# Attention with a GELU layer on one core: exponentials of later sets laid out by key block, value tiles cut at 224 queries, and a plan with new lengths

## The chip, the cores and the metric

The kernel runs on one core of a Trainium2 chip. The metric is the device time of one execution in microseconds (us); the median of nine runs before the change is 333.05 us (332.61 to 334.46). The core's engines work side by side, each with its own queue of instructions in order: TensorE (PE) multiplies matrices, VectorE (DVE) and ScalarE (ACT) work elementwise, GpSimd (POOL) applies masks and issues most loads, SyncE (SP) issues stores. An engine waits for another by a semaphore. Results of TensorE land in PSUM, which has eight banks of 512 four-byte columns on each of 128 partitions; this kernel gives four to scores and four to a ring that all other products share.

## The reference

`q`, `k`, `v` have 8 batches, 8 heads, 576 queries and 64 features; 16 "beacon" keys and values stand ahead of the 576 keys.

```python
k_all = np.concatenate([beacon_k, k], axis=2)          # 592 keys
v_all = np.concatenate([beacon_v, v], axis=2)
scores = np.matmul(q, k_all.transpose(0, 1, 3, 2)) / sqrt(64)
causal[:, 16:] = np.triu(np.ones((576, 576), dtype=bool), k=1)
scores = np.where(causal, -1000000000.0, scores)
a = np.exp(scores - scores.max(-1, keepdims=True))
a /= a.sum(-1, keepdims=True) + 1e-09
attn = np.matmul(a, v_all)                              # joined to (4608, 512)
h = x @ w_in                                            # (512, 2048)
g = h * (1.0 / (1.0 + np.exp(-1.702 * h)))
out = g @ w_out                                         # (2048, 512)
```

## The kernel before

**Sets.** Four heads of one batch make a *set*; there are 16 (`NSET`), two to a batch. Set s uses four 32-row or 32-column parts of TensorE at once, one for each head. The 592 keys are cut in five *blocks* of 128 (the last has 80). By causality block j concerns queries from `s0s[j]` = 0, 112, 240, 368, 496 on, so a head has 576 + 464 + 336 + 208 + 80 = 1664 columns of exponentials.

**Exponentials.** They lie in `E` (4 heads x 1664 columns) in the order of `PIECES`: first all blocks for queries 0 to 287, then all blocks for queries 288 to 575. The columns are computed in *chunks* of up to 512 (`CHUNKS`): scores (`e_qk`, L429, op `qk`), one ScalarE exponential for each set in it (`e_exp`, L447). There is a single score buffer, so chunk i+1 is computed once chunk i has been read. The triangles on the diagonal are masked in place (`e_mask`, L457; mostly on GpSimd). Sets 0 to 3 (`s < EARLY`) take their chunks by halves of queries; later sets run through the 1664 columns 512 at a time, a chunk often holding the end of one set and the start of the next.

**Sums and values.** For a later set VectorE adds the blocks' exponentials up (`e_zadd`, L484: six adds into `zs`), and a matmul with ones makes row sums (tile x = 2 of `e_av`, L504). Their reciprocal is made by transpose, reciprocal, transpose (`e_z1`, `e_z2`, L532 and L537). Values are matmuls of `E` with every second feature of `v` (x = 0 and 1), one tile for each x and half of the queries, and `e_norm` (L550) multiplies a tile with the reciprocals into `xT`. A set so opens six ring banks: two of sums and four of values. `avS.x.half` names these tiles.

**The GELU layer.** Groups of 256 (groups 0 and 1) and 512 tokens (groups 2 to 9) are multiplied with `w_in` (`e_m1`, L566, op `m1`), one ring bank for each tile. Groups 0 and 1 use a tanh on ScalarE and a gate on VectorE (L607); from group 2 on a GELU table is loaded on ScalarE (L598), and back for the next exponential. Groups 2 to 9 multiply with `w_out` by seven products of quarters (`e_prod`, L677, op `m2`), with sums of quarters on VectorE (`e_s`; `e_t` for the weights, op `t`) and joins (`e_join`, L704); groups 0 and 1 directly (`e_m2`, L619).

**The order.** `Plan` (L28) is a list scheduler that runs while the kernel is built: each operation has an engine, a length written in the kernel, a priority, and for some a due time; `LAT` is the time from an engine's end to another's start. It takes operations in order of the simulated time, and `choose` (L191) selects among TensorE's. `QUOTAS` says how many chunks must have been planned before the first products of a group may begin; `NEAR` lets VectorE wait for an urgent operation. Only the resulting order is in the program: on the chip each engine runs its list as soon as its semaphores allow. Loads of `q`, `k` and `v` are issued from GpSimd's queue, between the masks (`pool_load`, L730); `turns` (L777) transposes a set's queries and keys on VectorE; `values` (L832) and `mlp` (L1000) record the rest.

Of the kernel before, what the change touches and what calls it, by code (L numbers as in the profile page):

```python
# [13 lines left out]
NEAR = 260  # L14
# [9 lines left out]
class Plan:  # L24
# [3 lines left out]
    LAT = {"PE": 230, "ACT": 100, "DVE": 135, "POOL": 60, "Q": 1400, "SP": 0}  # L28
# [35 lines left out]
    def run(self):  # L64
# [33 lines left out]
        while todo:  # L98
# [23 lines left out]
            t, e = best  # L122
            ok = []
# [48 lines left out]
            for u in o.users:  # L172
                u.left -= 1
                lat = self.LAT[o.eng] if u.eng != o.eng or o.eng in ("Q", "DVE", "POOL", "ACT") else 0
                if u.eng == "Q":
                    lat = 300 if o.eng == "SP" else 1200
                elif o.name == "bk" and o.eng != "DVE":
                    lat = 2500
                u.ready = max(u.ready, o.end + lat)
                if u.left == 0:  # L180
                    avail[u.eng].append(u)
# [3 lines left out]
    def choose(self, ok, t, mode, last, free, inside):  # L185
# [15 lines left out]
        late = first(("av",), lambda o: o.ready + 6000 <= t)  # L201
# [11 lines left out]
def kernel(  # L213
# [51 lines left out]
    QUOTAS = (20, 26, 32, 41, 48, 55, 55, 55)  # L265
# [45 lines left out]
    def where(j, a):  # L311
        for (jj, qa, qe), col in zip(PIECES, ecol):
            if jj == j and qa <= a < qe:
                return col + a - qa

    DVM = (0, 1, 2)
    EARLY, ZSUM = 2 * HS, 2 * HS
# [97 lines left out]
    def qk_pieces(i):  # L415
        got, o = [], 0
        for (s, c0, c1) in CHUNKS[i]:
            for (j, a, e), col in zip(PIECES, ecol):
                u, v = max(c0, col), min(c1, col + e - a)
                if u < v:  # L420
                    got.append((v - u, s, j, a + u - col, o))
                    o += v - u
# [34 lines left out]
    def e_mask(s, j, a, e, eng):  # L457
        w = e - a
        col = where(j, a)
# [22 lines left out]
    ZW = HF - Z0  # L482

    def e_zadd(s, i):  # L484
        E = Es[s]
        if s not in zsum:
            zsum[s] = zp.tile([P, Q, ZW + HF], F16, tag="zs", name="zs")
        t = zsum[s]
        if i == 0:
            o, w, x, y = 0, ZW, E[:, :, Z0:HF], E[:, :, ecol[1] : ecol[1] + ZW]  # L490
        elif i == 1:
            w = HF - s0s[2]
            o = ZW - w
            x, y = t[:, :, o : o + w], E[:, :, ecol[2] : ecol[2] + w]
        elif i == 2:
            o, w, x, y = ZW, HF, E[:, :, ecol[3] : ecol[3] + HF], E[:, :, ecol[4] : ecol[4] + HF]
        else:
            j, a, e = PIECES[i + 2]
            w = e - a
            o = ZW + HF - w  # L500
            x, y = t[:, :, o : o + w], E[:, :, ecol[i + 2] : ecol[i + 2] + w]
        nc.vector.tensor_tensor(out=t[:, :, o : o + w], in0=x, in1=y, op=ALU.add)  # L502

    def e_av(s, x, half):  # L504
        b, hs = divmod(s, HS)
        u = ring_tile(("av", s, x, half))
        E = Es[s]
        q0 = half * HF
        terms = []
        if x == 2 and s >= ZSUM:  # L510
            if half == 0:
                terms.append((P, Z0, HF, zsum[s], 0, True, True))
                terms.append((P, 32, Z0, E, 32, True, True))
                terms.append((P, 0, 32, E, 0, True, True))
            else:
                terms.append((P, 0, HF, zsum[s], ZW, True, True))
        else:
            n = len(AVP[half])
            for i, (j, a, e) in enumerate(AVP[half]):
                terms.append((min(P, NK - j * P), a - q0, e - q0, E, where(j, a), i == 0, i == n - 1, j))  # L520
        for kw, a, e, src, col, first, last, *j in terms:
            for h in range(Q):
                lhs = ones[0:kw, :] if x == 2 else vb[b % NB2][0:kw, j[0], Q * hs + h, x::2]
# [8 lines left out]
    def e_z1(s, half):  # L532
        zt = zp.tile([P, HF], F32, tag="zt", name="zt")
        zs[(s, half)] = [zt]
        nc.vector.transpose(out=zt[:, :], in_=rings[("av", s, 2, half)][:, 0:HF])  # L535

    def e_z2(s, half):  # L537
        zt = zs[(s, half)][0]
        rc = zp.tile([P, HF // 32], F32, tag="rc", name="rc")
        nc.vector.reciprocal(  # L540
            out=rc[:, :], in_=zt[:, :].rearrange("p (b k) -> p b k", k=32)[:, :, 0]
        )
        rz = zp.tile([P, HF], F32, tag="rz", name="rz")
        nc.vector.transpose(
            out=rz[:, :].rearrange("p (b k) -> p b k", k=32),
            in_=rc[:, :].rearrange("p (b o) -> p b o", o=1).to_broadcast([P, HF // 32, 32]),
# [3 lines left out]
    def e_norm(s, x, half):  # L550
        b, hs = divmod(s, HS)
        t0 = (b * S + half * HF) % XR
        nc.vector.tensor_tensor(  # L553
            out=xT[:, 2 * hs + x, t0 : t0 + HF],
            in0=rings[("av", s, x, half)][:, 0:HF],
            in1=zs[(s, half)][1][:, :],
# [162 lines left out]
    T_ATT0, T_ATT1 = 13000, 245000  # L719
# [57 lines left out]
    def turns(s):  # L777
        urgent = s < HS
        cast = op(
            "DVE", 80, ld_bk[s] + [turn.get((s - 2, 1))], lambda: e_bk(s),  # L780
# [3 lines left out]
        for which in (1, 0):  # L784
            deps = [ld_qk[(s, which)], cast if which else None]
            turn[(s, which)] = op(
                "DVE", 1095 + 140 * which, deps + [qks[i] for i in CH_OF.get(s - NB2, [])],
                lambda which=which: e_turn(s, which),
                pr=0 if urgent else 4, due=max(0, due_of(s) - 9000), name=f"turn{s}",
            )  # L790

    def chunk(i):
# [14 lines left out]
        for n, (s, c0, c1) in enumerate(CHUNKS[i]):  # L807
            x = exps[(i, n)] = op(
                "ACT", 140 + 0.833 * 4 * (c1 - c0), [qks[i]], lambda n=n: e_exp(i, n), pr=0, name=f"exp{s}.{i}",
# [3 lines left out]
            for m, (j, a, e) in enumerate(MASKS):  # L813
                col = where(j, a)
                if c0 < col + e - a <= c1:
                    eng = "DVE" if s < HS and m in DVM else "POOL"
                    d = 130 + 4 * (e - a) / 1.92 if eng == "DVE" else 270 + 0.71 * 4 * (e - a)
# [10 lines left out]
    zseq += [(s, h ^ (s >= ZSUM)) for s in range(HS, NSET) for h in range(2)]  # L828
# [5 lines left out]
    def values(s):  # L834
        b, hs = divmod(s, HS)
        whole = s >= ZSUM
        order = [(2, 1), (2, 0), (0, 0), (1, 0), (0, 1), (1, 1)] if whole else [
# [4 lines left out]
        if whole:  # L842
            for i, w in enumerate((ZW, HF - s0s[2], HF, HF, S - s0s[3], S - s0s[4])):
                if i in (0, 2):
                    cols = [(ecol[i], ecol[i] + HF), (ecol[i + 1], ecol[i + 1] + HF)]
                    if i == 0:
                        cols = [(Z0, HF), (ecol[1], ecol[2])]
                    else:
                        cols = [(ecol[3], ecol[4]), (ecol[4], ecol[5])]
                else:  # L850
                    k = 2 if i == 1 else i + 2
                    cols = [(ecol[k], ecol[k] + w)]
                sums.append(
                    op(
                        "DVE", 80 + 0.55 * 4 * w, [x for u, v in cols for x in after(s, u, v)] + sums[-1:],
                        lambda i=i: e_zadd(s, i), pr=3, name="zadd",
                    )
                )
        for n, (x, half) in enumerate(order):
            deps = after(s, 0, ETOT) if whole else after(s, half * EHALF, ETOT if half else EHALF)  # L860
            if x < 2:
                deps += [vload[(b, j)] for (j, _, _) in AVP[half]] + [vload[(b, -1)]] + old
                deps += [z2[h] for h in range(2) if whole]
                deps += [avs[(s, 2, half)]]
            w = [e - a for (_, a, e) in AVP[half]]
            if x == 2 and whole:
                deps += sums
                w = [HF] if half else [ZW, Z0 - 32, 32]
# [6 lines left out]
            )  # L875
            if x == 2:
                z1 = op("DVE", 410, [avs[(s, x, half)]], lambda h=half: e_z1(s, h), pr=0, closes=key, name="z1")
                z2[half] = op("DVE", 600, [z1] + [norms.get((*two_back(s, half), y)) for y in range(2)], lambda h=half: e_z2(s, h), pr=0, name="z2")
            else:
                norms[(s, half, x)] = op(  # L880
                    "DVE", 380, [avs[(s, x, half)], z2[half]], lambda x=x, half=half: e_norm(s, x, half),
# [40 lines left out]
    SQ, SDVE, TDUE = 2, 0, 65000  # L922

    def weights():
        prev = []
        for i in range(4):
            prev = [op("DVE", 1450, w2_ld + (prev if i < 3 else [tds[0]]), lambda i=i: e_t(i, "DVE"), pr=3, due=TDUE, name="t")]
# [4 lines left out]
    def products(g):  # L932
        eng = "POOL" if g < SDVE else "DVE"
        sd = {}
        for n0 in range(0, HN, SQ):
            n1 = n0 + SQ
            prev = []
            for i in range(4):
# [3 lines left out]
                d = 150 + 1.0 * 256 * SQ if eng == "POOL" else 70 + 0.675 * 256 * SQ  # L942
# [25 lines left out]
        def join(p, src, dst, deps=(), closes=True):  # L968
            return op(
                "DVE", 620, [last[p]] + list(deps), lambda: e_join(g, p, src, dst), pr=2,  # L970
# [7 lines left out]
        half = op("ACT", 560, [last[1], ends.get(g - 1)], lambda: e_half(g, 1, "m"), pr=1, closes=("p", g, 1), name="half")  # L978
# [19 lines left out]
    def mlp(g):  # L998
# [5 lines left out]
        for hb in range(t0 // HF, (t1 - 1) // HF + 1):  # L1004
            b, half = divmod(hb, 2)
            for hs in range(HS):
                for x in range(2):
                    xs.append(norms[(HS * b + hs, half, x)])
# [5 lines left out]
        for n0 in firsts:  # L1014
# [7 lines left out]
            if g >= GEL:  # L1022
                gates[(g, n0)] = op(
                    "ACT", 555, [pe], lambda n0=n0, n1=n1: e_gelu(g, n0, n1),
# [3 lines left out]
            a = op("ACT", 555, [pe], lambda n0=n0, n1=n1: e_tanh(g, n0, n1), pr=1, name="tanh", table="e")  # L1028
            gates[(g, n0)] = op(
                "DVE", 610, [a], lambda n0=n0, n1=n1: e_gate(g, n0, n1), pr=2, closes=key, name="gate"  # L1030
# [4 lines left out]
        for mt in range(w // P):  # L1035
# [10 lines left out]
            ev = op("ACT", 560, [prev], lambda g=g, mt=mt: e_evac(g, mt), pr=1, closes=key, name="evac")  # L1046
# [61 lines left out]
```

## Time and profile before

| | us |
|---|---|
| median of nine runs | 333.05 |
| the profiled execution: its own time | 333.51 |
| its span in the profile | 331.8 |
| PE busy, of the span | 311.7 (94%) |
| DVE, ACT, POOL busy | 239.9, 202.9, 117.2 |
| 0 to 20 us: PE, DVE busy | 8.2, 11.7 |
| 20 to 68 us: PE, DVE busy | 45.3, 35.7 |
| 68 to 110 us | 41.2, 37.1 |
| 110 to 160 us | 49.7, 41.7 |
| 160 to 215 us | 55.0, 47.9 |
| 215 to 265 us | 49.4, 40.2 |
| 265 to 331.8 us | 62.9, 25.5 |

The profile shows one execution. A group is all instructions of one line and shape, with busy time, mean length of one in ns, and the idle time ahead of them with the engine that ended it. "L439" is a line of the kernel. A timeline row gives start, length, engine, line, operation, tile and count; matmuls overlap, so from row to row the starts say more than the lengths. The granted clock of TensorE is full in the whole span (0.998). The attention ends at 265 us; the rest is the last groups' products.

### The profile page before, as it was taken

The page shows a single profiled execution, that of the slowest core. Times are in us where ns is not written, and L with a number is a line of the kernel's source. Part 1 is how long each engine was busy: PE and PEld are TensorE (multiplying, and loading weights), DVE is VectorE, ACT ScalarE, POOL GpSimd, SP SyncE. Part 2 cuts the span into 40 slices and gives each one's busy share as a digit, 9 for nine tenths or more (in the row PEclk, how much of TensorE's full clock was granted, in tenths as well). Part 3 has the DMA queues.
Part 4 walks back from the last instruction along what each step waited for, and adds up shares of the span by engine and source line. Part 5 has one row for each costly group of instructions (what it writes and reads, how often), then busy time and mean ns, then how long its engine had stood idle before and what let it go on. Part 6 is the DMA issues. An engine that isn't in the chain of part 4 may idle for free.

```text
span 331.8 us, 10414 instructions
## 1 busy us (share of the span) xinstructions
PE 311.7 (94%) x4552; PEld 215.2 (65%) x4552; DVE 239.9 (72%) x514; ACT 202.9 (61%) x234; POOL 117.2 (35%) x190
## 2 busy tenths in 40 slices
PE   0599898999999999999999999999999999999995
PEld 0476566544786468645888888557865546846884
DVE  3846957898799779977899688977988600460483
ACT  1585586776866776778668576957676465065000
POOL 8765675382154606640556044702430000000000
PEclk9999999999999999999999999999999999999999
DMA  7999999449052915390449501920020000210122
GB/s 123 161 205 208 201 177 188 67 61 155 2 114 91 113 33 105 77 166 3 60 95 156 112 34 45 186 16 2 34 97 2 2 0 2 71 60 0 64 96 95
DMA packets 58221, 28.85 MB, mean 87 GB/s; under 512 B 41280, under 2 KB 53568, under 8 KB 58176
## 3 DMA queue, kind: packets, MB, share of 16 engines
q0 software_dynamic: 47552, 18.49, 47.4%
q1 hardware_dynamic: 10560, 9.69, 9.0%
q8 instruction: 35, 0.57, 0.7%
q14 instruction: 10, 0.08, 0.1%
q10 hardware_dynamic: 64, 0.01, 0.0%
HBM read 37.22 MB, written 9.44 MB: 141 GB/s over the span
## 4 chain that ended last, share of the span: by engine, by line
PE 70%; DMA 10%; issue 7%; POOL 5%; ACT 4%; DVE 3%; POOLq 0%; DVEq 0%
PE u L577 29%; PE u L691 25%; PE u L524 7%; PE s L439 6%; DMA w<-in_moe_w_in_dram 5%; DMA w<-in_moe_w_out_dram 5%; ACT E L450 3%; PE u L622 3%; POOL E L471 1%; DVE osb L707 1%; DVE zs L502 1%; POOL vb L370 1%; ACT L598 1%; POOL kn L354 1%; POOL qn L354 1%
## 5 line engine op out<-in xcount | busy, mean ns | idle before, releaser
L577 PE MATMUL u<-xT,w 128*128 128x512 f16 (+1 forms) x704 | 130.7, 342 | 1.5 <-ACT g L598 1.1
L450 ACT ACTIVATE E<-s 128x2048 f16<-128x2048 f32 (+4 forms) x66 | 98.8, 1514 | 51.1 <-PE s L439 50.4
L577 PEld LDWEIGHTS <-w 128*128 128x128 f16 x704 | 67.4, 98 | 57.0 <-issue 2.6
L598 ACT ACTIVATE g<-u 128x512 f16<-128x512 f32 x128 | 74.4, 599 | 46.0 <-PE u L577 31.7
L471 POOL TENSOR_SCALAR_AFFINE_SELECT E<-E 128x512 f16<-128x512 f16 (+3 forms) x90 | 52.6, 611 | 120.2 <-ACT E L450 118.2
L707 DVE SCALAR_TENSOR_TENSOR osb<-u,osb 128x512 f32<-128x512 f32 x56 | 37.7, 681 | 39.7 <-issue 26.5
L691 PEld LDWEIGHTS <-g 128*128 128x128 f16 x512 | 48.8, 98 | 7.0
L439 PE MATMUL s<-qT,kT 32*128 32x32 f16 (+9 forms) x1544 | 35.7, 226 | 13.2 <-DVE qT L410 11.8
L439 PEld LDWEIGHTS <-kT 32*128 32x128 f16 x1544 | 28.7, 95 | 27.7 <-issue 15.2
L691 PE MATMUL u<-w,g 128*128 128x256 f16 x384 | 46.0, 273 | 0.0
L691 PEld LDWEIGHTS <-sA 128*128 128x128 f16 x384 | 36.1, 98 | 5.3
L691 PE MATMUL u<-tB,sA 128*128 128x256 f16 x256 | 32.2, 273 | 0.0
L502 DVE TENSOR_TENSOR zs<-zs,E 128x192 f16<-128x192 f16 (+3 forms) x48 | 27.6, 574 | 3.1 <-POOL E L471 1.5
L524 PE MATMUL u<-E,vb 128*32 128x288 f16 (+4 forms) x1024 | 28.5, 257 | 0.3 <-DVE xT L553 0.3
L370 POOL DMA_DIRECT2D vb<-in_v_dram x32 | 27.3, 867 | 3.6 <-DMA kn<-in_k_dram 1.8
L553 DVE TENSOR_TENSOR xT<-u,rz 128x288 f16<-128x288 f32 x64 | 26.0, 449 | 1.7 <-PE u L524 1.2
L410 DVE STREAM_TRANSPOSE kT<-kn 128x576 f32<-128x576 f32 x16 | 20.1, 1257 | 6.8 <-DMA kn<-in_k_dram 3.2
L524 PEld LDWEIGHTS <-vb 128*32 128x32 f16 (+1 forms) x1024 | 21.9, 98 | 4.6 <-issue 1.7
L642 DVE TENSOR_TENSOR sA<-g 128x512 f16<-128x512 f16 x32 | 13.1, 427 | 14.5 <-ACT g L598 14.5
L410 DVE STREAM_TRANSPOSE qT<-qn 128x576 f32<-128x576 f32 x16 | 19.9, 1244 | 0.9 <-PE s L439 0.5
L535 DVE STREAM_TRANSPOSE zt<-u 128x288 f32<-128x288 f32 x32 | 13.9, 463 | 7.0 <-PE u L524 6.7
L502 DVE TENSOR_TENSOR zs<-E 128x704 f16<-128x704 f16 (+1 forms) x24 | 16.4, 682 | 1.3 <-POOL E L471 1.1
(44 smaller groups left out, 230.7 us busy)
## 6 DMA issues: line engine op xcount, KB each, us to landing
out_dram<-osb SPq DMA_DIRECT2D x36, 256.0 KB, 2.5
kn<-in_k_dram POOLq DMA_DIRECT2D x16, 288.0 KB, 6.5
qn<-in_q_dram POOLq DMA_DIRECT2D x16, 288.0 KB, 6.1
vb<-in_v_dram POOLq DMA_DIRECT2D x24, 128.0 KB, 5.6
w<-in_moe_w_in_dram POOLq DMA_DIRECT2D x8, 256.0 KB, 8.7
w<-in_moe_w_out_dram POOLq DMA_DIRECT2D x4, 512.0 KB, 14.0
vb<-in_v_dram POOLq DMA_DIRECT2D x8, 112.0 KB, 4.7
vb<-in_v_dram POOLq DMA_DIRECT2D x8, 80.0 KB, 5.7
```

What stands on the lines that cost most here:

```text
L370: nc.gpsimd.dma_start(out=t[0 : hi - lo, j, h0:h1, :], in_=v[b, h0:h1, lo:hi, :].rearrange("h n d -> n h d"),)
L410: nc.vector.transpose(out=f32(dst.rearrange("p n e -> p (n e)")).rearrange("p (r t) -> p t r", t=TR), in_=f32(src[:, :]).rearrange("p (t c ...
L439: nc.tensor.matmul(sc[:, h, o : o + w], kT[s % NB2][r : r + 32, j * P : (j + 1) * P, d], qT[s % NB2][r : r + 32, a : a + w, d], start=(d = ...
L450: nc.scalar.activation(out=Es[s][:, :, c0:c1], in_=ss[i][:, :, o : o + c1 - c0], func=AFT.Exp, scale=0.125,)
L471: nc.gpsimd.affine_select(out=blk, in_=blk, compare_op=ALU.is_ge, fill=0.0, base=off + (Nb if j == 0 else 0), pattern=[[0, Q], [1, w]], ch ...
L502: nc.vector.tensor_tensor(out=t[:, :, o : o + w], in0=x, in1=y, op=ALU.add)
L524: nc.tensor.matmul(u[32 * h : 32 * h + 32, a:e], lhs, src[0:kw, h, col : col + e - a], start=first, stop=last,)
L553: nc.vector.tensor_tensor(out=xT[:, 2 * hs + x, t0 : t0 + HF], in0=rings[("av", s, x, half)][:, 0:HF], in1=zs[(s, half)][1][:, :], op=ALU. ...
L577: nc.tensor.matmul(u[:, o + a - t0 : o + e - t0], w1t[:, kp, nt * P : (nt + 1) * P], xT[:, kp, a % XR : (e - 1) % XR + 1], start=(kp == 0) ...
L598: nc.scalar.activation(out=gts[g][:, n0:n1, 0:w], in_=rings[("m1", g, n0)][:, 0 : n * w].rearrange("p (n w) -> p n w", n=n), func=AFT.Gelu ...
L691: nc.tensor.matmul(u[:, HM * mt : HM * (mt + 1)], lhs[:, n, mt * P : (mt + 1) * P], rhs[:, n, :], start=(n == 0 and mt == 0), stop=(n == H ...
L707: nc.vector.scalar_tensor_tensor(out=osbs[(g, dst)][:, :], in0=rings[("p", g, p)][:, :], scalar=scale_of(g), in1=osbs[(g, src)][:, :], op0 ...
```

## The change

Sets 4 to 15 lay `E` out by block over all queries they concern (`WPIECES`: 576, 464, 336, 208 and 80 columns). The masks of a set are five (`WMASKS`) instead of six, the adds of the sums four instead of six, each over a block's whole width. The queries are cut at 224 (`HA`) instead of 288 for sums and values; for queries 0 to 223 the two value tiles (x = 0 and 1, 224 columns each) share one bank and one `e_norm`, for 224 to 575 they are tiles of 352 columns. A set so opens five banks. In the plan, lengths and latencies are other numbers, no latency is counted between operations of one engine, the first products of a group may begin ahead of the quota when TensorE would idle over 800 ns, and quotas, due times and `NEAR` change.

```diff
-NEAR = 260
+NEAR = 500
+IDLE = 800
...
-    LAT = {"PE": 230, "ACT": 100, "DVE": 135, "POOL": 60, "Q": 1400, "SP": 0}
+    LAT = {"PE": 230, "ACT": 178, "DVE": 212, "POOL": 110, "Q": 1400, "SP": 0}
...
+            if e == "PE" and not inside and t > free[e] + IDLE and group in self.quota:
+                f = firsts[group]
+                if f.left == 0 and f.ready <= t:
+                    inside = True
+                    continue
...
-                lat = self.LAT[o.eng] if u.eng != o.eng or o.eng in ("Q", "DVE", "POOL", "ACT") else 0
+                lat = self.LAT[o.eng] if u.eng != o.eng or o.eng == "Q" else 0
...
-        late = first(("av",), lambda o: o.ready + 6000 <= t)
+        late = first(("av",), lambda o: o.ready + 7000 <= t)
...
-    QUOTAS = (20, 26, 32, 41, 48, 55, 55, 55)
+    QUOTAS = (19, 28, 38, 42, 48, 55, 55, 55)
...
+    HA = 224
+    WPIECES = [(j, s0s[j], S) for j in range(NJ)]
+    WMASKS = [(j, s0s[j], s0s[j + 1] if j + 1 < NJ else S) for j in range(NJ)]
+    WMASKS[0] = (0, 0, s0s[1])
+    WAVP = [[(0, 0, HA), (1, s0s[1], HA)], [(j, max(HA, s0s[j]), S) for j in range(NJ)]]
...
+    def pieces(s):
+        return list(zip(PIECES, ecol)) if s < EARLY else list(zip(WPIECES, wcol))
...
+    def halves(s):
+        return ((0, HF), (HF, S)) if s < EARLY else ((0, HA), (HA, S))
...
     def e_zadd(s, i):
         E = Es[s]
         if s not in zsum:
-            zsum[s] = zp.tile([P, Q, ZW + HF], F16, tag="zs", name="zs")
...
+            zsum[s] = zp.tile([P, Q, S - Z0], F16, tag="zs", name="zs")
+        a = s0s[i]
+        t = zsum[s][:, :, a - Z0 :]
+        nc.vector.tensor_tensor(
+            out=t,
+            in0=E[:, :, Z0:S] if i == 1 else t,
+            in1=E[:, :, wcol[i] : wcol[i] + S - a],
+            op=ALU.add,
+        )
+
+    def av_terms(s, x, half):
+        E = Es[s]
+        q0 = halves(s)[half][0]
+        if x == 2 and s >= EARLY:
+            if half:
+                return [[2, P, 0, S - HA, zsum[s], HA - Z0, True, True, 0]]
+            return [
+                [2, P, Z0, HA, zsum[s], 0, True, True, 0],
+                [2, P, 32, Z0, E, 32, True, True, 0],
+                [2, P, 0, 32, E, 0, True, True, 0],
+            ]
+        blocks = (AVP if s < EARLY else WAVP)[half]
+        got = []
+        for n, (j, a, e) in enumerate(blocks):
+            got.append([x, min(P, NK - j * P), a - q0, e - q0, E, where(s, j, a), n == 0, n == len(blocks) - 1, j])
+        if s >= EARLY and half == 0:
+            got[-1][7] = False
+            second = [list(t) for t in got]
+            for t in second:
+                t[0], t[2], t[3], t[6] = 1, t[2] + HA, t[3] + HA, False
+            second[-1][7] = True
+            got += second
+        return got
...
+        n = 2 if s >= EARLY and half == 0 else 1
         nc.vector.tensor_tensor(
-            out=xT[:, 2 * hs + x, t0 : t0 + HF],
-            in0=rings[("av", s, x, half)][:, 0:HF],
-            in1=zs[(s, half)][1][:, :],
+            out=xT[:, 2 * hs + x : 2 * hs + x + n, t0 : t0 + w],
+            in0=rings[("av", s, x, half)][:, 0 : n * w].rearrange("p (n w) -> p n w", n=n),
+            in1=zs[(s, half)][1][:, 0:w].rearrange("p (o w) -> p o w", o=1).to_broadcast([P, n, w]),
             op=ALU.mult,
         )
...
-    T_ATT0, T_ATT1 = 13000, 245000
+    T_ATT0, T_ATT1 = 17000, 249000
...
-                "DVE", 1095 + 140 * which, deps + [qks[i] for i in CH_OF.get(s - NB2, [])],
+                "DVE", 1090 + 245 * which, deps + [qks[i] for i in CH_OF.get(s - NB2, [])],
                 lambda which=which: e_turn(s, which),
-                pr=0 if urgent else 4, due=max(0, due_of(s) - 9000), name=f"turn{s}",
+                pr=0 if urgent else 4, due=max(0, due_of(s) - 12000), name=f"turn{s}",
...
-                "ACT", 140 + 0.833 * 4 * (c1 - c0), [qks[i]], lambda n=n: e_exp(i, n), pr=0, name=f"exp{s}.{i}",
+                "ACT", 65 + 0.8345 * 4 * (c1 - c0), [qks[i]], lambda n=n: e_exp(i, n), pr=0, name=f"exp{s}.{i}",
...
-        order = [(2, 1), (2, 0), (0, 0), (1, 0), (0, 1), (1, 1)] if whole else [
+        order = [(2, 1), (2, 0), (0, 0), (0, 1), (1, 1)] if whole else [
...
-                    "ACT", 555, [pe], lambda n0=n0, n1=n1: e_gelu(g, n0, n1),
+                    "ACT", 480, [pe], lambda n0=n0, n1=n1: e_gelu(g, n0, n1),
```

The other edits are of the same kinds: lengths of masks, adds, norms, gates, joins and weight sums in the plan, the due time of the weight sums (65000 to 60000), and the lists of operations that `mlp` waits for, which follow the new cut of the queries.

## The prediction

> **What bounds the kernel now.** I read the page's busy times and slices first, then TensorE's waits, then its timeline at each wait, and last the groups of the operations that change.
>
> ```profile
> PE 311.7 (94%) x4552; PEld 215.2 (65%) x4552; DVE 239.9 (72%) x514; ACT 202.9 (61%) x234; POOL 117.2 (35%) x190
> ...
> PE   0599898999999999999999999999999999999995
> ...
> DVE  3846957898799779977899688977988600460483
> ```
>
> TensorE (PE) is busy from 8.5 us to the end; no other engine is. Only two things can move the time: less work in PE's own stream, or fewer gaps in it. The waits of PE add up to little:
>
> ```profile
> PE s L439 <- DVE qT L410: 11.8, 3, 8.5
> PE s L439 <- ACT E L450: 1.4, 4, 0.6
> PE u L577 <- ACT g L598: 1.1, 3, 0.4
> PE u L524 <- issue: 0.9, 1, 0.9
> PE u L577 <- DVE xT L553: 0.4, 1, 0.4
> PE u L524 <- DVE xT L553: 0.3, 1, 0.3
> PE u L622 <- DMA w<-in_moe_w_out_dram: 0.2, 1, 0.2
> ```
>
> Most of the first row is the start, which the change leaves alone (sets 0 to 3 keep their layout). The columns are total us, times, longest. The ends of matmuls are modelled, so I size each later gap by start-to-start times in PE's timeline:
>
> ```profile
> 35.57 0.64 PE L439 MATMUL s<-qT,kT 32*128 32x288 f16 x24 [0.80 <-DVE qT L410]
> ...
> 37.19 1.07 PE L577 MATMUL u<-xT,w 128*128 128x256 f16 x8 [0.36 <-DVE xT L553]
> ...
> 39.96 1.02 PE L622 MATMUL u<-w,g 128*128 128x512 f16 x4 [0.23 <-DMA w<-in_moe_w_out_dram]
> ...
> 61.80 0.68 PE L524 MATMUL u<-E,vb 128*32 128x288 f16 x20
> 62.41 1.04 PE L622 MATMUL u<-w,g 128*128 128x512 f16 x4
> 63.88 0.64 PE L439 MATMUL s<-qT,kT 32*128 32x288 f16 x24 [0.43 <-ACT E L450]
> ```
>
> ```profile
> 104.18 3.63 PE L577 MATMUL u<-xT,w 128*128 128x512 f16 x16
> 108.15 2.10 PE L577 MATMUL u<-xT,w 128*128 128x512 f16 x9 [0.34 <-ACT g L598]
> ```
>
> ```profile
> 136.86 0.68 PE L524 MATMUL u<-E,vb 128*32 128x288 f16 x20 [0.28 <-DVE xT L553]
> ```
>
> The reader is to see four kinds of gap. (1) Before 40 us: waits for a late transpose, a norm and the weights. (2) A score chunk waits for the exponential of the chunk before, since there is one score buffer: 61.22 to 63.88 is 2.66 us from chunk to chunk, the least that a 512-column chunk allows. (3) The first GELU of a group waits for ScalarE's table: four banks are filled (16 matmuls, 104.18 to 108.15 = 3.97 us, of which 16 x 0.216 = 3.46 is work), so 0.51 us is lost. (4) A value tile waits for a bank (0.44 us by starts).
>
> **The change, part by part.** Durations are those of the profiled execution, 333.51 us (span 331.8 and 1.7 around it), 0.46 above the median of 333.05.
>
> *PE's stream.* Score matmuls go from 1544 to 1376 and value matmuls from 1344 to 1248, at the same columns (212,992 and 267,264, counted from the program). Four heads run side by side, so columns set the time: a chunk of 24 score matmuls took 0.57 us (195.05 to 195.62) and one of 32 took 0.58 (203.57 to 204.15). Value tiles: 64 matmuls took 1.55 us at 3,328 columns a head; 56 at the same columns save between nothing and 8 x 24 ns = 0.19 us a set; columns being what counts, I take 0.01, some 0.1 for twelve sets. Runs of one kind go from 148 to 146, at about 0.1 us a switch. Together **-0.2 us**, ends 0 and -2.5.
>
> *Other engines.* VectorE's sums go from six adds a set (546+276+818+872+741+408 ns in the groups, 3.66 us) to four; by the slopes between those rows 1856 elements take about 1.25 us and 1344 about 0.95, so 3.35 with the two that stay. The joint norm saves one start, about 0.1 us. Over twelve sets VectorE loses some 5 us of 239.9; GpSimd has five masks for six (706 ns for 427+572), 3.5 us less. Both lie beside PE: after 68 us PE waited for VectorE once, for 0.3 us, and GpSimd spent 118.2 us waiting for ScalarE. I take nothing. If that cover went, 5 us of VectorE work could show, in neither direction proven by a row.
>
> *Wide adds against masks.* The 512-element mask has a mean of 706 ns over 30, at all overlaps that occur now; I take no change on the path, because a set's value sums stand at least one chunk (2.66 us) behind its last exponential in the order. The Trainium skill ("SBUF — State Buffer", section "Who interferes with whom") says that a VectorE instruction with two SBUF inputs locks out a GpSimd one that reads SBUF, which fully blocks until the first has ended; that speaks against replacing adds of 0.5 and 0.8 us by one of 1.25. By that rule alone a mask could wait 1.25 us a set: still inside the 2.66 us, hence nothing on PE, and 15 us on GpSimd's 35% load.
>
> *Before 40 us.* Gaps by starts now: 29.84 to 33.60 holds 3.46 us of work and a 0.1 switch (0.2 lost); 0.9 at 35.57; 0.45 at 37.19; 0.39 at 39.96: 1.94 us. In the changed order chunk 8 (the 35.57 one) stands behind a value tile, two tiles of group 0's second product and two first-product tiles of group 1, 0.54 + 2 x 0.86 + 2 x 0.87 = 4.0 us more; its transposes move behind a reciprocal chain, two norms and a gate on VectorE, about 1.7 us. So that wait goes, the norm at 37.19 gets a product tile (0.86 us) as cover, and two more first-product tiles (1.74 us) precede the third quarter of the output weights, which landed at 39.9. What is late next: two of the four banks are held by group 0's products, so the third tile of group 1 needs the first one's bank, whose gate (0.68) now stands behind set 3's key transpose (0.20 + 1.26) on VectorE: I work out 0.8 us. And two masks of set 1 slide behind two norms at 15 us: 0.25 us later for the first products. -1.94 + 0.8 + 0.25 = **-0.9**; ends 0 (all given back) and -1.94.
>
> *Up to group 2.* Gone: 0.07 at 51.84 and 0.15 at 53.35. New: group 2's first product follows set 3's last values with only chunk 18 between, 0.1 for the norm; 0.06 at chunk 15. **-0.1**; ends -0.22 and the second rival's price. The 0.87 us "issue" gap at 55.95 has no semaphore; I leave it in, its removal (-1.0) being a lower end.
>
> *Score cadence.* The 0.5 at 63.88 stays (chunk 17, three value tiles, chunk 18: 0.58 + 60 x 0.027 = 2.19 of 2.66). New: between chunks 25 and 26 stand only set 5's values, 0.58 + 1.54 = 2.12, so **+0.54**; behind the waiting chunk PE's whole queue stands still, since group 3's products follow it. Gone: at 244.89 (**-0.28**), where a fourth product piece now stands between.
>
> *Table waits.* Now 0.57 (71.76), 0.51 (108.15), 0.06, 0.15 and 0.53 (249.47): 1.82. In the changed order three groups (2, 3, 6) start directly behind a chunk, 3 x 0.51 = 1.53; at 4, 5 and 7 product or value tiles fill the 0.51. **-0.3**. The twelve table loads stay (1283 ns each).
>
> *Bank wait at 136.86.* A set now opens three value tiles instead of four after the sums, so the first norm frees the next bank in time: **-0.44**.
>
> *Lengths, latencies, quotas, due times, NEAR, IDLE* cost nothing themselves: they act through the order counted above. Loads that move in GpSimd's queue (query and key loads of sets 8, 10, 12 behind masks, of set 15 behind six value loads, about 5 us; one of set 4 ahead of masks) have 10 us and more: set 6's went out at 61.84 and was transposed at 74.61. If that cover were gone, a chunk would wait for its transpose as at 35.57, 0.9. SP's queue keeps its order. The tail after PE (joins, last store) stays.
>
> Sum: -0.2 - 0.9 - 0.1 + 0.54 - 0.28 - 0.3 - 0.44 = -1.68. Since the order is new at most places and each of the three gaps I find added was visible only by walking it, I keep 0.4 for one more of the same size (0.06 to 0.8). **-1.28 us**: 332.2 for an execution like the profiled one, 331.8 beside the median of 333.05.
>
> **The rivals.**
> *Given back early.* Group 1's tiles depend on VectorE's queue; if the third and fourth tile both wait behind transposes (0.8 each), the early part gains nothing and the sum is about -0.4: 332.6. For: VectorE is busy 35.7 of the 48 us from 20 to 68. Against: it still idles 12.3 us there.
>
> *Slower: the weight sums in front of group 2.* VectorE's order has two sums of the output weights (rows of 1.21 and 1.65 us) directly before the last reciprocal chain of set 3, and PE has nothing but chunk 18 before group 2's first product. If VectorE reaches them less than 2.9 us before set 3's sums leave PE, the norms are late by up to 2.9 us: 331.8 + 2.9 = 334.7; it decides from a VectorE lag of about 1.7 us on, the slack I count between the earlier chain and those sums. Against: before, the same sums ran at 65 to 72 us with no PE wait for VectorE.
>
> *More than forecast.* All early gaps go (-1.0 further) and the "issue" gap too (-1.0): 329.8.
>
> *It does not do what it says* cannot be: the counts of adds, masks and tiles fall in the built program; only their effect is open.
>
> **How the numbers follow.** Forecast 0.45 (own range 330.8 to 332.4), given back 0.2, slower 0.25 (from 333.7 to about 335), more 0.1. A measurement tells about 0.2% (0.67 us) from no change: faster is below 332.4: the forecast's 0.45 and the 0.1; same is the 0.2, slower the 0.25. The range from 330.4 to 334.3 leaves out half of "more" and two fifths of "slower", and holds the unknown bounds of the stream and the early part.
>
> **What would show it.** Right: PE busy near 311, its gaps at 35 to 40 us gone but one near 38 us behind a gate; a 0.5 us wait before chunk 26 (near 105 us) that was not there; table waits at groups 2, 3 and 6 only; no bank wait in the value tiles. VectorE near 235, GpSimd near 114. Wrong: a wait of group 2's first product for a norm near 66 us, chunk waits for transposes, or a new kind of gap after 110 us, where I count none.

## The result, and the profile after

The changed kernel takes 332.07 us (median of nine runs, 331.78 to 332.22). The kernel before takes 333.21 us (29 runs, the first nine among them). The ratio is 0.9964, with a 95% interval from 0.9954 to 0.9973: about 1.2 us faster. The forecast was 331.8 us, in a range of 330.4 to 334.3.

The profiled execution of the changed kernel took 332.22 us (span 330.5); that of before took 333.51 (span 331.8). First the page's busy times after:

```profile
PE 311.3 (94%) x4288; PEld 210.5 (64%) x4288; DVE 237.2 (72%) x478; ACT 203.5 (62%) x234; POOL 116.8 (35%) x178
```

TensorE is still the only engine that is busy nearly all the time, and its own work is 0.4 us less. VectorE lost 2.7 us and GpSimd 0.4 us, both less than the 5 and 3.5 that the prediction worked out. The waits of TensorE after (waiting line, engine and line waited for; total us, times, longest):

```profile
PE s L458 <- DVE qT L429: 11.1, 2, 8.6
PE s L458 <- ACT E L469: 1.4, 3, 0.6
PE u L604 <- DVE g L637: 1.1, 1, 1.1
PE u L604 <- ACT g L625: 1.0, 3, 0.4
PE u L545 <- DVE zs L508: 0.5, 1, 0.5
PE u L649 <- DVE xT L580: 0.3, 1, 0.3
```

Four rows of before are gone: the 0.9 us "issue", the value tile and the first product that waited 0.3 and 0.4 us for a norm, and the 0.2 us for the output weights. Three are new: a first product (L604) that waits 1.1 us for a gate (L637), a sum tile (L545) that waits 0.5 us for an add (L508), and a second product (L649) that waits 0.3 us for a norm (L580). In the timeline of TensorE after, at the places that the prediction spoke of:

```profile
34.46 1.02 PE L649 MATMUL u<-w,g 128*128 128x512 f16 x4 [0.26 <-DVE xT L580]
...
38.03 0.64 PE L458 MATMUL s<-qT,kT 32*128 32x288 f16 x24
...
39.74 1.91 PE L604 MATMUL u<-xT,w 128*128 128x256 f16 x16 [1.08 <-DVE g L637]
...
66.15 0.66 PE L458 MATMUL s<-qT,kT 32*128 32x336 f16 x24 [0.39 <-ACT E L469]
...
102.75 0.64 PE L458 MATMUL s<-qT,kT 32*128 32x448 f16 x16 [0.34 <-ACT E L469]
103.32 3.63 PE L604 MATMUL u<-xT,w 128*128 128x512 f16 x16
107.28 2.96 PE L604 MATMUL u<-xT,w 128*128 128x512 f16 x13 [0.33 <-ACT g L625]
...
208.47 0.38 PE L545 MATMUL u<-zs,ones 128*32 128x352 f16 x8 [0.46 <-DVE zs L508]
```

The score chunk at 38.03 waits for nothing: the transpose wait of before is gone. The gate wait at 39.74 is the new early gap, and 102.75 is the new wait between two score chunks. Group 3 still waits for ScalarE's table: 103.32 to 107.28 is 3.96 us for 3.46 of work. The gap at 208.47 was in no list of mine. VectorE's timeline after shows who made the first and the last of these wait:

```profile
37.91 1.25 DVE L429 STREAM_TRANSPOSE kT<-kn 128x576 f32<-128x576 f32 x1
39.01 1.27 DVE L637 SCALAR_TENSOR_TENSOR g<-sig,u 128x512 f16<-128x512 f16 x2
...
206.41 0.58 DVE L508 TENSOR_TENSOR zs<-zs,E 128x832 f16<-128x832 f16 x1
206.91 1.28 DVE L734 SCALAR_TENSOR_TENSOR osb<-u,osb 128x512 f32<-128x512 f32 x2
208.10 0.31 DVE L508 TENSOR_TENSOR zs<-zs,E 128x320 f16<-128x320 f16 x1
```

Set 3's key transpose stands ahead of two gates, and two joins stand between the third and the last add of set 12's sums.

**Where the time went.** I sized every gap of TensorE by start-to-start times, from 20 us on, against the usual pitch of the instruction ahead. "Run n" is the n-th uninterrupted run of score matmuls; the four points are places to which the two orders have done the same work, as far as the steady difference around them tells.

| from 20 us up to (start before, after) | gaps before | gaps after | difference, running sum | start after less start before |
|---|---|---|---|---|
| run 26 (103.61, 102.75) | 4.39 | 3.36 | -1.03 | -0.85 |
| run 34 (154.35, 152.95) | 1.01 | 0.50 | -1.54 | -1.40 |
| run 41 (190.87, 189.70) | 0 | 0.28 | -1.26 | -1.17 |
| last matmul (327.63, 326.39) | 0.96 | 0.99 | -1.23 | -1.24 |

The listed gaps are as large as the gain at the last matmul (1.23 and 1.24 us), but that they match so well is in part chance. At run 5 both orders have done the same matmuls, and there the changed kernel is 0.65 us behind (22.89 against 22.23). From run 5 to the last matmul it takes 1.89 us less, 0.66 more than the gaps; 0.47 of this falls between run 5 and run 26. I did not find it in single places; a shorter stream may be part of it.

The late start scatters by itself: run 5 began between 21.76 and 22.89 us in the eleven profiles of this case, and 22.89 is the latest. During the start-up TensorE's matmuls take longer than later, and they do so for longer in the profile of the changed kernel than in that of before. Here is the fourth run of scores, the same 32 matmuls, first after, then before:

```profile
20.25 0.82 PE L458 MATMUL s<-qT,kT 32*128 32x208 f16 x32
```

```profile
19.90 0.55 PE L439 MATMUL s<-qT,kT 32*128 32x208 f16 x32
```

The granted clock that the profile gives, full over the whole span, does not show this. Since the two executions differ in it, what the two masks do there, the only work that the change moves at the start, can't be read from them.

### The profile page after: what moved, and what is told of

It is laid out like the page before. It is cut to its first block, busy times and chain, and to the rows that moved or that the text cites. A ratio compares the mean times of both kernels' runs of the same rounds, so it can differ in the third digit from the quotient of the medians.

```text
span 330.5 us, 9837 instructions
## 1 busy us (share of the span) xinstructions
PE 311.3 (94%) x4288; PEld 210.5 (64%) x4288; DVE 237.2 (72%) x478; ACT 203.5 (62%) x234; POOL 116.8 (35%) x178
## 5 line engine op out<-in xcount | busy, mean ns | idle before, releaser
L604 PE MATMUL u<-xT,w 128*128 128x512 f16 (+1 forms) x704 | 130.5, 342 | 2.1 <-DVE g L637 1.1
L604 PEld LDWEIGHTS <-w 128*128 128x128 f16 x704 | 67.7, 98 | 58.5 <-issue 3.2
L458 PE MATMUL s<-qT,kT 32*128 32x32 f16 (+20 forms) x1376 | 36.0, 235 | 12.5 <-DVE qT L429 11.1
L458 PEld LDWEIGHTS <-kT 32*128 32x128 f16 x1376 | 26.0, 96 | 29.9 <-issue 15.1
L718 PE MATMUL u<-tB,sA 128*128 128x256 f16 x256 | 31.3, 273 | 0.0
L545 PE MATMUL u<-E,vb 128*32 128x352 f16 (+8 forms) x928 | 27.7, 267 | 0.0
L580 DVE TENSOR_TENSOR xT<-u,rz 128x352 f16<-128x352 f32 (+2 forms) x52 | 24.9, 518 | 1.7 <-PE u L545 1.1
L508 DVE TENSOR_TENSOR zs<-zs,E 128x1344 f16<-128x1344 f16 (+2 forms) x36 | 23.4, 650 | 3.1 <-POOL E L490 0.5
L545 PEld LDWEIGHTS <-vb 128*32 128x32 f16 (+1 forms) x928 | 20.1, 99 | 5.4 <-issue 1.3
L557 DVE STREAM_TRANSPOSE zt<-u 128x352 f32<-128x352 f32 (+2 forms) x32 | 13.8, 459 | 8.9 <-PE u L545 8.8
L718 PE MATMUL u<-tB,g 128*128 128x256 f16 x128 | 16.3, 273 | 0.0
```

Of the source, the lines that this page charges most:

```text
L458: nc.tensor.matmul(sc[:, h, o : o + w], kT[s % NB2][r : r + 32, j * P : (j + 1) * P, d], qT[s % NB2][r : r + 32, a : a + w, d], start=(d = ...
L508: nc.vector.tensor_tensor(out=t, in0=E[:, :, Z0:S] if i == 1 else t, in1=E[:, :, wcol[i] : wcol[i] + S - a], op=ALU.add,)
L545: nc.tensor.matmul(u[32 * h : 32 * h + 32, a:e], lhs, src[0:kw, h, col : col + e - a], start=first, stop=last,)
L580: nc.vector.tensor_tensor(out=xT[:, 2 * hs + x : 2 * hs + x + n, t0 : t0 + w], in0=rings[("av", s, x, half)][:, 0 : n * w].rearrange("p (n ...
L604: nc.tensor.matmul(u[:, o + a - t0 : o + e - t0], w1t[:, kp, nt * P : (nt + 1) * P], xT[:, kp, a % XR : (e - 1) % XR + 1], start=(kp == 0) ...
L718: nc.tensor.matmul(u[:, HM * mt : HM * (mt + 1)], lhs[:, n, mt * P : (mt + 1) * P], rhs[:, n, :], start=(n == 0 and mt == 0), stop=(n == H ...
```

## The experiments

Two theories stood at first. By the *gap theory* the time follows the sum of TensorE's gaps, which the order of instructions sets; layout and plan act only through that order. By the *load theory* the lighter VectorE and GpSimd (fewer adds and masks) buy the time, so that the layout alone should bring it. The kernel before had medians of 333.17, 333.53 and 333.19 us beside the three groups of runs; each ratio below is against the runs beside it.

**The plan's numbers without the layout.** Sets keep the old pieces, adds and six banks; lengths, latencies, `IDLE`, `NEAR`, quotas and due times are those of after. The tile `zt` gets a third buffer of its own pool.

```diff
-NEAR = 260
+NEAR = 500
+IDLE = 800
...
-    LAT = {"PE": 230, "ACT": 100, "DVE": 135, "POOL": 60, "Q": 1400, "SP": 0}
+    LAT = {"PE": 230, "ACT": 178, "DVE": 212, "POOL": 110, "Q": 1400, "SP": 0}
...
+    ztp = ctx.enter_context(tc.tile_pool(name="ztp", bufs=3))
...
-    QUOTAS = (20, 26, 32, 41, 48, 55, 55, 55)
+    QUOTAS = (19, 28, 38, 42, 48, 55, 55, 55)
...
-        zt = zp.tile([P, HF], F32, tag="zt", name="zt")
+        zt = ztp.tile([P, HF], F32, tag="zt", name="zt")
```

> The layout of before (pieces by halves, six adds, four value tiles) with the lengths, latencies, quotas, due times, NEAR and IDLE of after; the transposed sums get a third buffer, without which this order would stand still. Gap theory (the time is the sum of TensorE's gaps, and the order that the plan's numbers give sets these): TensorE's order up to chunk 20 is that of after, so group 3 begins as early as in after, about 0.85 us ahead of before; later the order differs: table waits 1.0 us in place of 1.8, chunk waits 1.8 in place of 1.0. Together 0.3 to 1.4 us faster than before (331.8 to 332.9). Load theory (the gain is the layout's lighter VectorE and GpSimd): no faster than before, 333.2.

Measured: 338.22 us, ratio 1.0153 [1.0138, 1.0168]. This is a clear miss, 5 us above what I expected. Up to run 20 TensorE's order is that of after, and at run 26 it stood 0.56 us ahead of before; so the early gain comes from the plan's numbers. Behind that, ten gaps from 89 us on add up to 6.3 us (by starts), and the last matmul starts 4.8 us later than before's. Most are waits for a ring bank or a norm; the largest, 1.31 us at 172.27, names no semaphore. Two of the waits in TensorE's timeline of this kernel:

```profile
200.85 1.03 PE L698 MATMUL u<-tB,sA 128*128 128x256 f16 x8 [1.01 <-DVE xT L560]
...
245.84 0.68 PE L531 MATMUL u<-E,vb 128*32 128x288 f16 x20 [0.62 <-DVE osb L714]
```

A product piece waits for a norm to free its bank, and a value tile for a join. So the plan's numbers are worth something early and cost 1.5% with six-bank sets behind.

**The layout without the plan's numbers.** All of the new layout, with before's lengths, latencies, quotas and due times, and without `IDLE`.

```diff
-NEAR = 500
-IDLE = 800
+NEAR = 260
...
-    LAT = {"PE": 230, "ACT": 178, "DVE": 212, "POOL": 110, "Q": 1400, "SP": 0}
+    LAT = {"PE": 230, "ACT": 100, "DVE": 135, "POOL": 60, "Q": 1400, "SP": 0}
...
-    QUOTAS = (19, 28, 38, 42, 48, 55, 55, 55)
+    QUOTAS = (20, 26, 32, 41, 48, 55, 55, 55)
```

> The layout of after (key blocks, cut at 224, shared bank) with the lengths, latencies, quotas, due times and NEAR of before and no IDLE. Gap theory: TensorE's order up to chunk 19 is that of before, so the waits before 40 us come back (a transpose near 35 us, a norm near 37); behind it four chunks stand too near to the one before (0.5 to 0.8 us each, 2.7 in place of 1.0), the table waits are 1.6 and the bank wait of 0.44 is gone: 0 to 1 us slower than before, 333.2 to 334.2. Load theory: it has the whole gain, about 332.1.

Measured: 334.79 us, ratio 1.005 [1.0037, 1.0064]. This is 0.6 us above the range that I expected. It has the lighter VectorE and GpSimd (235.4 and 113.3 us busy, less than after) and is slower than before: the load theory falls. The early gaps of before are back (0.37 at 35.39, 0.45 at 37.00, 0.39 at 39.77), and chunks follow too closely on one another in TensorE's timeline:

```profile
172.70 0.64 PE L452 MATMUL s<-qT,kT 32*128 32x448 f16 x16 [0.74 <-ACT E L463]
175.32 0.65 PE L452 MATMUL s<-qT,kT 32*128 32x400 f16 x24 [0.44 <-ACT E L463]
```

Neither part gives the gain; both together do. The question was then what of the layout the plan's numbers need.

**The shared bank undone.** After, but queries 0 to 223 get two value tiles and two norms again, so that a set opens six banks. Blocks, masks, adds and the plan's numbers stay.

```diff
-        if s >= EARLY and half == 0:
-            got[-1][7] = False
-            second = [list(t) for t in got]
...
-            got += second
...
-        n = 2 if s >= EARLY and half == 0 else 1
+        n = 1
...
-        order = [(2, 1), (2, 0), (0, 0), (0, 1), (1, 1)] if whole else [
+        order = [(2, 1), (2, 0), (0, 0), (1, 0), (0, 1), (1, 1)] if whole else [
```

> After, with the shared bank undone: the cut at 224 and the key blocks stay, but the two tiles of queries 0 to 223 have a bank and a norm each, so a set opens six banks. The plan arranges itself anew, with after's numbers; TensorE's order is that of after up to chunk 21. Bank theory (plan_only lost its 5 us because four value tiles fill the ring of four and wait for norms, which its plan did not see): value tiles wait again for norms and joins, 0.3 to 0.8 us in five or more sets, 2 to 5 us slower than after: 334 to 337. Rival (plan_only lost by the six narrow adds on VectorE): within 0.7 us of after, 331.4 to 332.8.

Measured: 336.98 us, ratio 1.0098 [1.0076, 1.012], 1.3% above after's ratio. Behind chunk 21 the plan makes another order. TensorE's timeline of this kernel:

```profile
134.72 0.60 PE L711 MATMUL u<-tB,sA 128*128 128x256 f16 x4 [0.56 <-DVE xT L573]
...
245.12 0.75 PE L538 MATMUL u<-E,vb 128*32 128x352 f16 x20 [0.85 <-DVE osb L727]
```

These are the same two kinds of wait as with the plan's numbers alone. Against after it is 0.25 us behind at run 26, 1.24 at run 32, 3.09 at run 54 and 5.03 at the last matmul. The waits for joins and norms that the profile names (0.34, 0.33, 0.56, 0.63 and 0.85 us) are 2.7 of that; I did not break down the rest, part of which is work that slid behind the attention. What is shown is that undoing the shared bank alone, with the order that the plan then makes, costs more than the whole change gains.

**The wide adds halved.** After, with each add wider than 232 columns made in two halves. The lists of TensorE and GpSimd stay as they are. This sets the gap theory against a *port theory*: that a wide add holds masks up, and that this costs time.

```diff
+        m = (a + S) // 2 if S - a > 232 else S
+        for u, v in ((a, m), (m, S)):
+            if u < v:
+                t = zsum[s][:, :, u - Z0 : v - Z0]
...
```

> After, with each add of the sums that is wider than 232 columns done in two halves one behind the other; TensorE's and GpSimd's lists are those of after. Gap theory: VectorE gets 24 more instructions, some 2 to 3 us in all, at places where TensorE does not wait, but the late add at 208.5 us comes 0.1 to 0.3 us later: 332.0 to 332.5. Port theory (a wide add holds masks up, and the sums wait for the masks): masks of 512 elements fall from a mean of 732 ns towards 706, the last add comes earlier and the wait at 208.5 shrinks: 331.6 to 332.0.

Measured: 332.22 us, ratio 0.9957 [0.9942, 0.9973], the same as after. Here is the group of the 512-element masks, first after and then with halved adds, where TensorE's timeline at set 12's sums follows:

```profile
L490 POOL TENSOR_SCALAR_AFFINE_SELECT E<-E 128x512 f16<-128x512 f16 x42 | 30.3, 732 | 105.4 <-ACT E L469 101.7 <-PE u L545 3.7
```

```profile
L490 POOL TENSOR_SCALAR_AFFINE_SELECT E<-E 128x512 f16<-128x512 f16 x42 | 28.9, 697 | 105.8 <-ACT E L469 102.2 <-PE u L548 3.5
```

```profile
208.80 0.38 PE L548 MATMUL u<-zs,ones 128*32 128x352 f16 x8 [0.82 <-DVE zs L511]
```

The masks do get shorter, from 732 to 697 ns. Those that overlap an add fall from a mean of 936 to 813 ns, beside 642 alone. It buys nothing, since GpSimd idles (35% busy); and the wait for set 12's last add grows from 0.53 to 0.89 us by starts, as two halves take longer than one add.

**The two largest new gaps, one by one.** The planned list is edited after planning: `nth` finds an operation by engine and name, and `put(x, y)` moves x behind y, or ahead of it with `False`; each engine keeps the rest of its list. Set 3's key transpose goes behind the first two gates of group 1 in VectorE's list:

```diff
+    key3 = nth("DVE", "turn3")
+    gate = [o for o in order[order.index(key3) :] if o.eng == "DVE" and o.name == "gate"]
+    put(key3, gate[1])
```

> After, with one change in VectorE's list: set 3's key transpose moves behind the first two gates of group 1. Gap theory: the wait of 1.1 us of the third product tile at 39.7 us goes, at most 0.2 is left, and what follows is 0.8 to 1.1 us earlier to the end: 331.0 to 331.3. Rival (before 40 us the stage is held by the arrival of the output weights, and VectorE's work is the same in any order): the wait moves to the weights or to another bank, the end moves by less than 0.3 us.

Measured: 331.42 us, ratio 0.9948 [0.9935, 0.9961]. The 1.15 us at 39.74 went; 0.20 at 40.40 and 0.51 at 42.26 came, behind the next gates, so the gain was about 0.5 us by the ratios where I had expected 0.8 to 1.1. The interval overlaps that of after, so the times alone leave it open; in the profiles, run 5 to the last matmul takes 0.42 us less than after. VectorE's and TensorE's timelines of this kernel:

```profile
37.44 0.68 DVE L637 SCALAR_TENSOR_TENSOR g<-sig,u 128x512 f16<-128x512 f16 x1
```

```profile
42.26 1.03 PE L604 MATMUL u<-xT,w 128*128 128x256 f16 x8 [0.34 <-DVE g L637]
```

And chunk 47 goes ahead of set 12's two sum tiles in TensorE's list:

```diff
+    put(nth("PE", "qk47"), nth("PE", "av12.2.1"), False)
```

> After, with one change in TensorE's list: set 12's two sum tiles stand behind chunk 47 and not ahead of it. Gap theory: the wait for the last add at 208.5 us (0.5) goes, the table wait at 213.4 (0.46) is filled by the sums, and chunk 47 waits 0.2 for the exponential ahead of it: 0.6 to 0.8 us faster than after, 331.3 to 331.5. Rival (the add is late because VectorE is behind, so TensorE waits for it wherever the sums stand): no more than 0.2 us.

Measured: 331.42 us, ratio 0.9953 [0.994, 0.9967]. The time lies in the range expected, but the gain does not: against after it is about 0.4 us by the ratios, where I had expected 0.6 to 0.8, and the intervals overlap. The chunk now waits 0.22 us by starts and the sums not at all; the table wait of group 6 (0.46) has become 0.37 for a join. From run 41 to the end this kernel gains 0.46 us on after. TensorE's timeline:

```profile
207.69 0.65 PE L458 MATMUL s<-qT,kT 32*128 32x336 f16 x24 [0.15 <-ACT E L469]
208.28 0.38 PE L545 MATMUL u<-zs,ones 128*32 128x352 f16 x8
```

**Both moves.**

```diff
+    put(key3, gate[1])
+    put(nth("PE", "qk47"), nth("PE", "av12.2.1"), False)
```

> After, with the moves of gates_first and sums_behind_chunk together. Gap theory: the two gaps lie 170 us apart and TensorE is full between them, so the gains add: 0.65 and 0.65 us, 330.6 to 331.0, a ratio to before of about 0.992. Rival (a gain ahead is given back where TensorE next meets the exponentials' or VectorE's pace): no faster than either alone, 331.4.

Measured: 330.93 us, ratio 0.992 [0.9902, 0.9937]. This is faster than both kernels: its interval lies below that of after (0.9954 to 0.9973). The halved adds, which measured the same as after, took 332.22 us in the same group of runs. Removing gaps by hand brings time as the gap theory has it. Whether the two moves add up is not shown: by the ratios it is 1.5 us against 0.5 and 0.4, and the intervals are too wide. In the profiled executions the last matmul starts no earlier than with the second move alone (325.45 and 325.47 us); there a gap of 0.50 us (by starts) stands where after has none, in the same order of TensorE:

```profile
27.44 0.82 PE L604 MATMUL u<-xT,w 128*128 128x256 f16 x6 [0.34 <-issue]
```

**The gap without a semaphore.** The prediction left before's gap at 55.95 us as it was; after, it is gone. First, before was profiled once more, unchanged:

> The kernel before, profiled a second time. If the gap of 1.0 us without a semaphore at 55.95 us belongs to this order of instructions, it is there again within 0.5 us of that place; if it was an accident of one execution, it is not, and the span is about 330.8.

Measured: one execution of 333.95 us. TensorE's timeline again has the gap, at the same instructions, 1.45 us by starts:

```profile
54.85 0.30 PE L524 MATMUL u<-E,ones 128*32 128x288 f16 x2
56.43 0.30 PE L524 MATMUL u<-E,ones 128*32 128x288 f16 x6 [1.28 <-issue]
```

It belongs to this program and is no accident of one execution. Second, in before, a product piece of group 1 goes ahead of set 3's first sum tile on TensorE:

```diff
+    tiles = [o for o in order if o.eng == "PE"]
+    first = next(o for o in tiles if o.name == "av3.2.0")
+    piece = next(o for o in tiles[tiles.index(first) :] if o.name.startswith("m2.1.0"))
+    order.remove(piece)
+    order.insert(order.index(first), piece)
```

> The kernel before, with one change in TensorE's list: the 0.86 us product piece that stands behind set 3's first value tiles (near 56.7 us) goes ahead of them. Order theory (the gap of 1.0 to 1.4 us without a semaphore at 55.95 us comes because two bursts of small matmuls use up the instructions that TensorE has at hand; a packet of the instruction queue landed 1.3 to 1.4 us ahead of its end both times): the piece gives the packet 0.86 us more, the gap shrinks to 0.2 to 0.6, and the time falls by 0.5 to 0.9 us, 332.3 to 332.7. Rival (something that set 3's sums wait for): the gap keeps its end at the same place and the time stays.

Measured: 332.82 us, ratio 0.999 [0.9981, 0.9999]: a gain too small to name. TensorE's timeline of this kernel:

```profile
54.15 0.60 PE L622 MATMUL u<-w,g 128*128 128x512 f16 x2
55.43 0.60 PE L622 MATMUL u<-w,g 128*128 128x512 f16 x2 [0.68 <-issue]
```

The gap has moved into the product piece, after as many matmuls as before (862), and is 0.84 us by starts; I had expected 0.2 to 0.6. In this order it goes with the place in TensorE's stream, not with set 3's sums or what they read.

## Why the prediction was right or wrong

The total was close (-1.24 us between the profiled executions, against -1.28) because errors of both signs cancelled. That is luck, and it goes beyond the table below, whose gaps begin at 20 us: the 0.65 us that the changed kernel was late at run 5 stand against 0.66 that no listed gap explains. Term by term, with gaps by starts:

| step of the prediction | forecast | measured |
|---|---|---|
| PE's stream | -0.2 | not isolated; -0.66 is not in the listed gaps |
| before 40 us | -0.9, of it +0.25 at 15 us | -0.46 (1.96 to 1.50) from 20 us on |
| 51.84 and 53.35 | -0.22, and 0.12 to 0.16 new | -0.22 |
| "issue" gap at 55.95, "I leave it in" | 0 | -1.04 |
| wait before chunk 26 | +0.54 | +0.43 |
| chunk wait at 244.89 | -0.28 | -0.28 |
| chunk wait at 63.88 | stays, 0.5 | stays, 0.48 |
| table waits | -0.3 | -0.34 (1.82 to 1.48) |
| bank wait at 136.86 | -0.44 | -0.44 |
| "0.4 for one more of the same size" | +0.4 | +1.15 |

**Right.** The table waits fell on groups 2, 3 and 6 and no others. The score cadence, the bank wait and the new wait before chunk 26 came where the walk through the new order had put them. The lighter load of VectorE and GpSimd did not buy the time: the layout alone, which has all of it, was slower than before. The four adds of a set take 1204, 932, 663 and 353 ns, 3.15 us in all against 3.35 worked out.

**"Before 40 us -0.9" was mis-sized by half.** From 20 us on the early gaps fell by 0.46 us. Two terms were too small. The gate behind set 3's key transpose cost 1.15 us, not 0.8; and a product waited 0.35 us for a norm at 34.46, where I had counted on cover. That is the rival "given back early" come true in part.

**"I leave it in" failed.** The 0.87 to 1.04 us without a semaphore were treated as fixed, with removal as a lower end. The gap came again in all four executions with before's early order, and in the changed kernel's profile none such comes after 20 us. This one step brought most of the gain, and I had no reason from the profile for either sign. Nor is the new order free of such gaps: with both moves one of 0.50 us stands at 27.44, under the same order of TensorE.

**"0.4 for one more" was too little.** Five small gaps (0.07 to 0.19) and the 0.53 at 208.47 were new; before's 0.09 at 97.7 went. The 0.53 was there to be found: VectorE's list of after has the two joins of 206.91 ahead of the last add, and TensorE's list has the sums behind little other work. I walked VectorE's list around set 3 but not around set 12.

**Wide adds against masks: nothing on the path, as forecast.** Masks of 512 elements that overlap an add take 936 ns in the mean instead of 642, and VectorE's 1856-element add 1336 ns beside a mask instead of 1110 alone. Which of the two grows depends on which began first. In six pairs in which one mask and one add overlap each other alone, by 0.28 to 0.60 us, the first keeps the shortest length of its shape within 0.02 us and the second grows by the overlap less 0.12 to 0.14. (In a seventh both begin within 0.02 us of each other, and the mask grows.) One of the six, where the add came second, from the timelines of GpSimd and VectorE:

```profile
156.92 0.63 POOL L490 TENSOR_SCALAR_AFFINE_SELECT E<-E 128x512 f16<-128x512 f16 x1 [10.67 <-ACT E L469]
```

```profile
156.95 1.58 DVE L508 TENSOR_TENSOR zs<-E 128x1856 f16<-128x1856 f16 x1 [0.40 <-ACT E L469]
```

The Trainium skill ("SBUF — State Buffer", section "Who interferes with whom") says that a VectorE instruction with two SBUF inputs contends with a GpSimd one that reads SBUF, that the port pair they share is an exclusive lock, and that issue order decides who blocks. This trace agrees. The prediction looked at the blocked mask only. The halved adds show that neither sets the time.

**The slower rival did not occur.** Group 2's first product followed chunk 18 without a wait for a norm; the weight sums did not delay it.

**Left out of the forecast:** that the two halves of the change depend on each other. With six banks a set, the same plan's numbers lose 1.0 to 1.5% against before. I had credited the shared bank with one wait (0.44 us), read off before's order; its worth in the new order is larger.

Still open: what TensorE waits for in the gap without a semaphore, the causes of the five small gaps, which the view of waits does not name, and where the 0.66 us outside the listed gaps lie.

## What to carry to other kernels

Where one engine is busy 94% of the time, list all its gaps by start-to-start times, then walk the new order of every engine that feeds it, to the end and not only around the edit: each gap moved by hand here gave about what it measured, less what the next wait took. When a change alters a layout and a planner's numbers together, run each alone, since neither need carry the gain. And count the ring banks that an operation opens: here the sixth bank of a set cost more than the whole change gained.

## What the runs showed of the hardware that was not expected

TensorE can stand still for 0.7 to 1.5 us with no semaphore to wait for. With before's early order it does so ahead of the 863rd matmul: 1.04 and 1.45 us in two executions of before, 0.67 in the layout alone, 0.84 in the piece that was moved there. With the plan's numbers alone 1.31 us stand at 172.27 us. In each of these a packet of 16 KB of the instruction queue had landed 1.29 to 1.39 us ahead of the end of the gap. In the seven executions with after's early order (`plan_only` and `six_banks` among them) the last packet had landed 2.9 to 3.7 us ahead of the 863rd matmul, and there is no gap at it; but 512 matmuls earlier four of the seven lose 0.16 to 0.50 us, 1.26 to 1.51 us behind a packet. Most packets have no gap behind them: the queue moved 35 in before and 33 after, whose program is shorter. That speaks for the fetching of instructions, but it is argued from the timing alone; no run took the fetch away.

Where a GpSimd mask and a VectorE add overlapped, the one that began second grew by all but 0.12 to 0.14 us of the overlap. It can be either, so a wide add can also be the one that waits: one of 1856 elements took 1.58 us beside a mask, 1.11 alone.
